# Batch 0's transposes in four PSUM banks instead of two, and a new order of all work (gated recurrence, then an MLP mixer, one core)

## The chip, the core and the metric

The kernel runs on one core of a Trainium2 chip. The metric is device time in microseconds, the median of several executions; lower is better. One further execution was recorded by the hardware profiler, and every row below comes from that one.

## What is computed

Four batches, eight heads, 768 steps, head width 48. First a recurrence with a decaying 48x48 state per head, then an MLP mixer over tokens and over channels:

```
for t in range(S):                                   # S = 768
    state = alpha[t, :, None] * state + outer(k[t], v[t])
    y[t]  = q[t] @ state
x  = y of all heads side by side                     # [4, 768, 384]
h  = relu(x^T @ w_tok1) @ w_tok2                     # w_tok1 768x256, w_tok2 256x768
u  = x + h^T
out = u + relu(u @ w_ch1) @ w_ch2                    # w_ch1 384x1536, w_ch2 1536x384
```

## The kernel before

**The recurrence by chunks.** A batch is cut into six chunks of 128 steps. The logarithm of alpha (`la`, on ACT) is summed along the chunk by matmuls (`cum`), the sums become two exponentials on ACT (`ek` and `eq`), and k and q are multiplied by them (`pkk` on POOL; `pkq` on DVE in batch 0 and on POOL later). TensorE (PE) transposes both (`tr`), the transposes are copied out of PSUM (`tp`, to the tiles `tk2`/`tq2` or `tkq`), and their products (`gt`) are masked on DVE (`gm`) and applied to v (`y`). The state of the chunk before comes in by `inter`, and the new state is made by `state`, `st` and `ss`. The result of a chunk is `x`. The three pairs of batch 0 and the first two pairs of batch 1 are "paired": two chunks at a time with interleaved steps. The other chunks are "natural": one at a time.

**The mixer.** `tok1` (L602 after batch 0) multiplies all six `x` by `w_tok1`, `ht` is its relu, `tok2` (L651) multiplies by `w_tok2`, `u` adds `x` on DVE, `utp` transposes and `ut` copies out. Batch 0 does this by another route (L582, L629, L634) that ends in `ut` as well. Then `ch1` (L691) makes 24 pieces of the hidden layer, `rt` is their relu, `ch2` (L715, three parts for each of six row blocks) brings them together, `o` copies out and `out` stores. The `ch1` and `ch2` of one batch are independent of the recurrence of the next batch, and they are put between its instructions.

**Weights.** All weights arrive in fp32 and are cast to bf16 by ACT, DVE or POOL: `wc1` in two halves of three casts each, `wc2` in four pieces (the casts are numbered 154, 156, 158, 160 in the table below).

**The order.** Nothing is scheduled at build time. Every piece of work gets a number when the graph is built, and the table `ORDER` lists these numbers in the order in which they are issued. A letter behind a number names the engine (A for ACT, D for DVE, P for POOL), the digits behind a dot are the PSUM banks, and `f` with a bank is a filler: one matmul of zeros, whose result nobody reads. The fillers all stand ahead of the first `ch1`. Each engine carries out its own instructions strictly in that order, so an instruction that waits holds back all behind it on its engine. Loads and stores are issued by SP, in the order of the table too.

**The transposes of batch 0.** For each pair and each of k and q there is one PSUM bank. The transposes of both chunks go into it, chunk `s` at column `512 * s`. Two copies take them out: of k one chunk each, of q two of the four head pairs of both chunks each. Of the two copies of one bank one goes to ACT and one to DVE. Between two engines that read the same bank a wait is placed.

Of the kernel before, what the change touches and what calls it, by code (L numbers as in the profile page):

```python
# [17 lines left out]
FUSE = 99  # L18
FETCH, BLOCK, AHEAD, ARRIVES = 193, 256, 449, (4.5, 30.0, 3.0)
# [6 lines left out]
0 1 f0 2 f0 f0 f0 f0 f0 3 f0 f0 f0 f0 f0 4 28 f0 29 f0 f0 30.0 5 31.1 32 f2 f2 38 6 f2 35 f2 33 f2 f2 f2 39 f2 34 f2  # L26
36 40 f2 43.2 41 7 f3 66 47.3 f4 65 48 44 49A 50D f4 67.4 46A 45D 68.5 69 f6 51.67 75 72 54.01 8 70 52 f3 f3 76 f3 73
f3 77 f3 80.3 78 f2 9 84.2 56 f6 85 105 81 71 f6 104 87D f6 f6 10 86A f6 f6 83D 106.6 82A 55 107.5 108 53 91.14 11 114
88.23 92 f0 42P 37A f0 f0 109 90 f0 58.07 115 89 57.13 60A 93 f2 116 12 f2 f2 59 f2 f2 f2 112 f2 111 63 61 117 14
123.2 64A f0 62 f0 124 74A 79P 119.0 110 16 120 125D 126A f4 94.41 122A 121D 18 96 127.57 97 130.36 95.20 128 113A  # L30
118P 100 132 98 102 133.4 99A 20 131 13P f5 103A 169.5 101 163.6 24 166.2 f3 15P 129 141.3 135 142.0 143 136 134.17
17P 137 139 145 138D 147 140A 144 146 259 148 150 149 151 19D 152 172.4 178.1 162A 161D 175.7 f0 173 176 174A 167 177D
260 164 168A 170 22D 21P 165A 179 f0 171A 23D f0 261 f0 180A f0 189.0 201.3 190A 195.4 262 202A 181.7 27D 25P 196A
185.2 26D 182A 153 193.6 186A 211.5 264 194D 223.1 263 212D 227.0 224A 265.3 228A 266.4 155 267 217.7 273 270 207.2
274 209.6 268 300 208D 218A 276 213.5 210D 215.1 214A 269 187.0 301 271 216A 203.4 188A 219.3 275 204A 302 225.2 220A
154D 199.7 272 226A 278.65 277 279 200A 303 221.1 280D 281A 156P 183.0 222A 282 283 184A 292.43 284D 285A 197.2 304
294 286.71 157 305 198D 289.05 205.6 287 306.4 288 206A 159 191.2 308 291 307.7 309 311 239.6 296 314 343 290 315
249.1 297 192D 293.54 344 312 319.37 298 295A 345 254.0 316 299A 234.2 158A 346 317 244.5 347 310 313 160D 240 318 348
245 351 241 349 320 352.4 242A 321D 246 322A 354 235 247D 353 350 358 236 356 243 323 362 324 237D 333.64 357 325A
326D 376.5 238 363.2 335 250 248 355 364 336 486 365 327.37 251 487 329 366 367 330.62 328 252A 488 255 332 368 256  # L40
339 369 359.73 331 257A 370.12 340 229.4 361A 360D 253 372D 371A 377 373.60 258 510 334.73 375 489 381.21 341 490 374
337 230 342A 378 382 338A 491 379.5 383 231 380A 492 384.0 232D 511.6 385A 493 513 388.3 512 516 233 386.2 389A 514
517 494 521 495 515 387D 522.7 390.1 496 523 398.5 391 524 394.4 526 396.0 399 392.6 395 400.3 527 535.2 393 518.17
401 497 402.54 528 519A 397 529.63 525 403A 553.1 404D 498 520A 536 405.05 530A 416.4 499 554 406A 440.7 407D 555 531A
500 417D 420.2 539 434.6 421D 441A 501 532.10 435A 550.53 534 422.4 502 430.2 551 546 423A 540.7 533 431A 452.6 558
552 442.0 541 537.5 453D 503 542 438.4 544 538D 559.2 439A 556.1 443D 504 560 543 412.3 545 557D 561 426.6 413D 505
432.7 564 427A 410.5 506 433A 446.4 562 411A 565 408.0 507 447A 563 572.1 577 450.2 409D 508 454.3 573 451A 547.67 574
455D 566.54 509 548A 578.0 549D 591.1 568A 567D 448.2 720 592 580 424.3 584 449D 579 588.76 583 721 425A 569.54 590
418.1 596 582 436.2 570 419A 414.0 571 437A 581 597.3 593 589 722 610.6 575.5 598 444.1 415D 599 601 723 576A 594.2
611 445A 481.4 595D 602 724 744 428.7 476.0 600 429A 725 603 604.35 612 585.61 605A 726 466.2 587D 586A 477 727 606A  # L50
482 728 607.73 751 615.16 609 483 729 755 616 471.5 608 478 617 613.3 730 479 472 614A 484 618.1 480 762 456.7 619D
473 485 773 622.6 731 474 732 620.0 623A 475 457 621A 733 458 734 634.3 459 630.4 735 628.1 635 632.5 631 624.6 780
460 626.0 629 461.7 625 792 736 627 462 737 633 463 636.34 738 464 639.16 637A 467 638D 640A 641D 465 468 799 774.0
469 745.5 775 793.7 656.4 746 778 747 756.3 470 650.6 795 739 757 749 684.1 651D 740 758 644.2 685D 776 748 662.5 794
760 645D 741 660.6 811 663D 657A 678.3 750 742 661D 787.0 769.1 679A 812.7 770 759 668.2 743 777 813 761 672.5 788 814
664.4 669A 673D 789 670.6 665A 666.3 779 671A 646.1 830 667D 682.0 798 647A 831.7 683A 806.2 781.54 797 832 807 763.63
833 752.10 765D 658.2 783A 835 754D 764A 674.7 753D 659D 782A 686.3 808 675D 800.40 687A 803.16 796 802D 816 784.25
801A 766.73 804 680.0 768 818 654.4 681A 836 767 648.1 655A 844.3 786 642.0 649A 817 771.7 785 822.41 643A 652.5 772A
805 834 837 790.2 824 815 653A 809.0 791A 823 838.76 810A 819.51 825.2 839D 820A 828.4 840D 676.0 821A 826 715.7 829D
827 677A 849.65 841.21 845 716 843 846 700.4 851 695.0 850 696 842 852.3 688.1 853D 847.5 689A 705.6 848D 697 854.2  # L60
698 699 717 855A 710.3 718 711 701 719 702 856.1 703 704 712 857A 690.5 713 858.0 714 868.2 859 862.7 860.4 869 864.1
863 866.3 691 861 867 692 865 706 693 873.02 694 870.74 874A 875D 707 871D 872A 910.3 708 894.1 911A 709 880.5 895A
908.2 881D 906.0 909A 912.7 907A 900.4 913A 876.6 901A 896.3 877A 918.1 897A 914.5 919D 904.2 915A 922.0 905D 902.7
923D 920.4 903A 898.6 921A 916.3 899A 888.1 917A 890.5 889A 884.2 891D 878.0 885A 886.7 879A 882.4 887A 892.6 883D
929.3 893A 939.1 930 931 940 932 944.5 933 945 946 934.2 947 941 948 924.0 942 925 943 926 935 927 936 928 949.7 937
950 938 951 954.4 955 952 956 953 957 958
# [12 lines left out]
class Graph:  # L79
# [5 lines left out]
    def add(self, name, costs, emit, reads=(), writes=(), prio=0, dma=None, new=(), tail=0.0, rows=False, loose=False, n=0, late=0.0):  # L85
        self.ops.append(Op(costs, emit, new))
        return self.ops[-1]
# [6 lines left out]
def kernel(  # L94
# [12 lines left out]
    nc = tc.nc  # L107
# [73 lines left out]
    gm_t = many("gm", 2 * NG, [128, 4, 128])  # L181
    ss_t = many("ss", NSS, [128, H, D])
    x_t = many("x", NX, [128, HD])
    ht_t = many("ht", 2 * NDT, [128, HD])
# [19 lines left out]
    def load_input(dst, src, service, keys, prio, loose=False):  # L204
        return g.add("load", {"SP": 0.06}, lambda e: nc.sync.dma_start(dst, src), writes=keys, prio=prio, dma=service, loose=loose)  # L205
# [629 lines left out]
```

## The time and the profile before

| | |
|---|---|
| time before, median of 3 | 174.6 us (173.99 to 174.98) |
| the profiled execution | 174.24 us, of which its span is 172.5 us |
| PE busy | 166.5 us (96%), 2099 matmuls, 61 of them fillers |
| DVE, ACT, POOL busy | 102.0, 96.0, 72.3 us |
| granted TensorE clock | 9 tenths or more in every slice |
| DMA | 9 tenths busy or more in most slices up to about 120 us |

A row of the timeline gives start, busy time, engine, line, operation, tiles written and read with their shapes, the count, and in brackets how long the engine had been idle and what released it. The busy time of a PE row reaches past the start of the next row, since matmuls overlap; how long a group holds PE is therefore read from the starts of two rows that follow each other.

### The profile page before, as it was taken

Reading aid. Unit: us, or ns where it says so; the run is one execution under the profiler, and the core shown is the slowest. Engines: PE = TensorE matmul, PEld = TensorE weight load, DVE = VectorE, ACT = ScalarE, POOL = GpSimd, SP = SyncE. Lnnn points to the kernel's source line nnn. Section 1 sums busy time; section 2 is a strip of 40 time slices with the busy share of each in tenths; the row PEclk is TensorE's granted clock in tenths of the full one; section 3 lists DMA queues with packets and bytes.
Section 4 is the critical chain, followed back from the end, with each engine's and each line's share of the span. In section 5 each row is a group of like instructions: output and inputs, shape, how many; then the busy total and the mean of one; then the engine's idle time right before and its main releaser. Section 6 shows DMA issues by size and latency. Waiting matters only on the chain.

```text
span 172.5 us, 5143 instructions
## 1 busy us (share of the span) xinstructions
PE 166.5 (96%) x2099; PEld 106.8 (62%) x2099; DVE 102.0 (59%) x212; ACT 96.0 (56%) x206; POOL 72.3 (42%) x114
## 2 busy tenths in 40 slices
PE   7999979999999999999999999999999999999993
PEld 3566656665666567566666665666676656656562
DVE  3159977544653597689593727495988248132231
ACT  2577552699865655497887231699771112865000
POOL 7252542319485782944877111499941000000000
PEclk9999999999999999999999999999999999999999
DMA  5999999999998999999999999995000221100133
GB/s 134 261 261 265 232 335 398 309 234 337 256 307 168 205 254 219 225 170 198 165 204 151 196 219 223 211 210 92 4 4 0 79 104 50 46 4 0 46 115 113
DMA packets 86150, 30.20 MB, mean 175 GB/s; under 512 B 79600, under 2 KB 85104, under 8 KB 86128
## 3 DMA queue, kind: packets, MB, share of 16 engines
q1 hardware_dynamic: 86128, 29.89, 75.2%
q8 instruction: 16, 0.26, 0.7%
q14 instruction: 6, 0.05, 0.1%
HBM read 25.17 MB, written 4.72 MB: 173 GB/s over the span
## 4 chain that ended last, share of the span: by engine, by line
PE 78%; DVE 6%; POOL 4%; DMA 3%; issue 3%; ACT 2%; SPq 1%; DVEq 0%; POOLq 0%
PE bank L691 27%; PE bank L715 23%; PE bank L289 4%; PE bank L651 3%; DMA ina<-in_alpha_dram 3%; PE bank L602 3%; DVE gm L309 2%; PE bank L387 2%; PE bank L338 2%; PE bank L423 2%; POOL pkk L275 2%; PE bank L521 1%; PE bank L411 1%; PE bank L352 1%; SPq L205 1%
## 5 line engine op out<-in xcount | busy, mean ns | idle before, releaser
L691 PE MATMUL bank<-ut,wc 128*128 128x384 bf16 x288 | 51.1, 326 | 0.0
L691 PEld LDWEIGHTS <-wc 128*128 128x128 bf16 x288 | 26.6, 98 | 16.5
L275 POOL TENSOR_TENSOR pkk<-ink,ek 128x384 bf16<-128x384 f32 x24 | 24.3, 1022 | 17.7 <-ACT ek L256 14.9
L715 PE MATMUL bank<-wc,rt 128*128 128x384 bf16 x144 | 26.5, 326 | 0.0
L715 PE MATMUL bank<-wc,rt_late 128*128 128x384 bf16 (+2 forms) x156 | 25.1, 314 | 0.0
L728 DVE TENSOR_TENSOR o<-bank,x 128x384 f32<-128x384 f32 (+2 forms) x19 | 10.1, 536 | 18.2 <-PE bank L715 18.2
L589 ACT ACTIVATE rt<-bank 128x384 bf16<-128x384 f32 x33 | 16.3, 494 | 7.4 <-PE bank L691 7.0
L282 POOL CAST vb<-inv 128x384 bf16<-128x384 f32 x21 | 10.5, 506 | 22.3 <-DMA inv<-in_v_dram 17.6
L715 PEld LDWEIGHTS <-rt_late 128*128 128x128 bf16 x156 | 14.4, 98 | 8.2
L275 POOL TENSOR_TENSOR pkq<-inq,eq 128x384 bf16<-128x384 f32 x18 | 17.9, 1003 | 2.8 <-ACT eq L258 2.8
L589 ACT ACTIVATE rt_late<-bank 128x384 bf16<-128x384 f32 x33 | 16.1, 495 | 5.3 <-PE bank L691 5.3
L309 DVE TENSOR_TENSOR gm<-bank,u 128x512 bf16<-128x512 f32 x28 | 17.3, 682 | 2.8 <-PE bank L387 2.6
L243 ACT ACTIVATE la<-ina 128x384 bf16<-128x384 f32 x24 | 12.1, 526 | 10.8 <-DMA ina<-in_alpha_dram 10.8
L715 PEld LDWEIGHTS <-rt 128*128 128x128 bf16 x144 | 13.2, 98 | 7.7
L792 PE MATMUL bank<-zeros 128*128 128x384 bf16 x61 | 15.1, 372 | 1.4 <-DVE la L192 1.2
L591 DVE TENSOR_SCALAR rt_late<-bank 128x384 bf16<-128x384 f32 x15 | 8.3, 554 | 10.0 <-PE bank L691 8.3
L309 DVE TENSOR_TENSOR gm<-bank,pmask 128x512 bf16<-128x512 f32 x20 | 12.7, 682 | 1.4 <-PE bank L521 1.3
L256 ACT ACTIVATE ek<-bank 128x384 f32<-128x384 f32 x24 | 11.4, 498 | 3.5 <-PE bank L355 2.0
L333 ACT CAST x<-bank 128x384 bf16<-128x384 f32 x16 | 7.3, 483 | 10.6 <-PE bank L338 9.4
L322 POOL TENSOR_TENSOR ss<-st,al 128x384 bf16<-128x384 f32 x12 | 10.0, 832 | 7.4 <-DVE st L319 5.4
L591 DVE TENSOR_SCALAR rt<-bank 128x384 bf16<-128x384 f32 x15 | 7.9, 554 | 5.3 <-PE bank L691 5.3
L297 ACT COPY tkq<-bank 128x512 bf16<-128x512 bf16 x17 | 9.3, 602 | 2.8 <-PE bank L289 2.7
(118 smaller groups left out, 237.3 us busy)
## 6 DMA issues: line engine op xcount, KB each, us to landing
out_dram<-o SPq DMA_DIRECT2D x23, 192.0 KB, 2.6
ina<-in_alpha_dram SPq DMA_DIRECT2D x14, 192.0 KB, 4.3
ink<-in_k_dram SPq DMA_DIRECT2D x14, 192.0 KB, 4.6
inq<-in_q_dram SPq DMA_DIRECT2D x14, 192.0 KB, 4.5
inv<-in_v_dram SPq DMA_DIRECT2D x14, 192.0 KB, 4.4
rt_late<-in_moe_w_ch_dram SPq DMA_DIRECT2D x2, 1152.0 KB, 10.1
rt_late<-in_moe_w_ch_dram SPq DMA_DIRECT2D x4, 576.0 KB, 7.1
ina<-in_alpha_dram SPq DMA_DIRECT2D x5, 384.0 KB, 6.3
```

Source lines behind the costliest of these rows:

```text
L243: g.add("la", {"ACT": 0.43}, lambda e: act.activation(la[:, :, 0:D], t, AF.Ln), key, [u["la"][1]], pr + 5)
L256: g.add("ek", {"ACT": 0.38}, lambda e: act.activation(ek, banks[bank.place][:, 0:HD], AF.Exp, scale=-1.0), [bank], [kek], pr + 4)
L275: lambda e, dst=dst, src=src, ex=ex: {"POOL": gps, "DVE": dve}[e].tensor_tensor(dst[:, :, 0:D], src, ex().rearrange("p (h d) -> p h d", h= ...
L282: lambda e: evict[e](vb, src), ksrc, [u["vb"][1]], pr + 4)
L309: g.add("gm", {"DVE": 0.60}, lambda e: dve.tensor_tensor(gm, banks[bank.place].rearrange("p (j t) -> p j t", j=4), wide(mask, [[0, 4], lis ...
L322: g.add("ss", {"POOL": 0.79}, lambda e: gps.tensor_tensor(ss, st.rearrange("p (h d) -> p h d", h=H), wide(al, [[1, 8], [0, D]]), ALU.mult) ...
L589: act.activation(dst, src, AF.Relu)
L591: dve.tensor_scalar_max(dst, src, 0.0)
L691: pe.matmul(banks[bank.place][:, 0:HD], lhsT=wc1[wp][:, kc, off : off + 128], rhs=ut_t[b % 2][:, kc, cs], start=(kc == 0), stop=(kc == NM ...
L715: pe.matmul(banks[bank.place][:, 0 : hi - lo], lhsT=rt_t[(b * NDC + mc) % NRT][:, i * 128 : i * 128 + 128], rhs=wc2[:, mc, lo:hi], start=( ...
L728: g.add("o", {"DVE": 0.09 + 0.38 * width}, lambda e, i=i, bank=bank, o=o, lo=lo, hi=hi: dve.tensor_tensor(o[:, lo:hi], banks[bank.place][: ...
L792: pe.matmul(banks[place][:, 0:HD], lhsT=zeros[:, 0:128], rhs=zeros, start=True, stop=True, skip_group_check=True)
```

## The change

**Four banks.** In batch 0 each half that is copied out on its own now has its own bank: two for k (one for each chunk) and two for q (one for each half of the heads). The number of transposes, copies and bytes stays the same. The copies of one pair no longer share a bank.

```diff
-                bank = Bank()
+                tb = [Bank(), Bank()]
                 for s in range(2):
                     src, ksrc = us[s]["p" + w]
...
                         for j in range(4):
-                            pe.transpose(ps[:, 512 * s + 128 * j :][:, 0:128], src[:, 2 * j : 2 * j + 2, :], id128)
-
-                    g.add("tr" + w, {"PE": 0.225}, emit, [ksrc], [bank], pr + 2, new=[] if s else [bank])
+                            part, at = (s, 128 * j) if w == "k" else (j // 2, 256 * s + j % 2 * 128)
+                            pe.transpose(banks[tb[part].place].bitcast(BF16)[:, at : at + 128], src[:, 2 * j : 2 * j + 2, :], id128)
+
+                    mine = [tb[s]] if w == "k" else tb
+                    g.add("tr" + w, {"PE": 0.225}, emit, [ksrc], mine, pr + 2, new=mine if w == "k" or s == 0 else [])
                 for part in range(2):
-                    def evicted(e, w=w, bank=bank, part=part):
+                    def evicted(e, w=w, part=part, bank=tb[part]):
                         ps = banks[bank.place].bitcast(BF16)
                         if w == "k":
-                            evict[e](tk2[:, part], ps[:, 512 * part : 512 * part + 512].rearrange("p (j t) -> p j t", j=4))
+                            evict[e](tk2[:, part], ps[:, 0:512].rearrange("p (j t) -> p j t", j=4))
                         else:
                             evict[e](tq2[:, 2 * part : 2 * part + 2].rearrange("p j (t s) -> p (j t) s", s=2),
-                                     wide(ps[:, 256 * part : 256 * part + 1], [[1, 256], [512, 2]]))
+                                     wide(ps[:, 0:1], [[1, 256], [256, 2]]))
```

**Switches that are off.** The change also brings uneven loads (`UNEVEN`), a `y` in two parts (`SPLIT`) and a mask by way of ACT and POOL (`AROUND`). All three lists are empty, so none of them issues anything. Their code moves the later lines by some 20.

**The order.** The whole table is another one. Two lines of it:

```diff
-36 40 f2 43.2 41 7 f3 66 47.3 f4 65 48 44 49A 50D f4 67.4 46A 45D 68.5 69 f6 51.67 75 72 54.01 8 70 52 f3 f3 76 f3 73
+40 f2 43.2 41 7 47.34 66 f5 34 f5 45D 65 48 44.5 50A 49D f6 67.6 46A 68.7 69 51.10 75 54.24 72 53 f3 8 70 f3 f3 76 55
```

There are 63 fillers now instead of 61, again all ahead of the first `ch1`. SP issues its first 38 loads in the same order as before, which is everything up to the end of batch 1's input; the stores of batch 0 then stand a little earlier among the loads of batch 2.

DVE in batch 0, the first pair and the start of the second (`tq20`, `tk20` are the transposes of the first pair, `tq21`, `tk21` of the second, `gm` the masks; L481 and L479 are the copies of q and k). Before:

```order
L481 COPY tq20_151<-bank3_64 128x512
L479 COPY tk20_153<-bank2_63 128x512
L309 TENSOR_TENSOR gm0_155<-bank6_67,pmask0_97 128x512
L275 TENSOR_TENSOR pkq2_121<-inq1_108,bank4_65 128x8x48
L275 TENSOR_TENSOR pkq3_122<-inq1_108,bank5_66 128x8x48
L309 TENSOR_TENSOR gm3_158<-bank1_62,pmask1_98 128x512
L265 TENSOR_TENSOR al2_137<-bank4_65,bm_84 128x16
L481 COPY tq21_152<-bank2_63 128x512
L479 COPY tk21_154<-bank3_64 128x512
```

And now, where the copies are L496 for k and L498 for q:

```order
L496 COPY tk20_153<-bank2_63 128x512
L498 COPY tq20_151<-bank3_64 128x512
L325 TENSOR_TENSOR gm1_156<-bank0_61,pmask0_97 128x512
L325 TENSOR_TENSOR gm2_157<-bank2_63,pmask1_98 128x512
L284 TENSOR_TENSOR pkq2_121<-inq1_108,bank6_67 128x8x48
L274 TENSOR_TENSOR al2_137<-bank6_67,bm_84 128x16
L284 TENSOR_TENSOR pkq3_122<-inq1_108,bank7_68 128x8x48
L325 TENSOR_TENSOR gm3_158<-bank4_65,pmask1_98 128x512
L325 TENSOR_TENSOR gm0_155<-bank1_62,pmask0_97 128x512
L496 COPY tk21_154<-bank2_63 128x512
```

The copy of k now goes ahead of that of q, and of the second pair DVE keeps one copy of four; ACT has the other three. In the third pair it is also one for DVE and three for ACT, instead of two and two.

ACT in batch 1, around the `la` of its fifth chunk (`la2` from `ina1`, L243 before and L252 now; `wc2` is the cast of the second channel weight, L762 and L782). Before:

```order
L333 CAST x6_172<-bank5_66 128x384
L333 CAST x7_173<-bank4_65 128x384
L762 CAST wc2_219<-rt_late_184 128x1152
L243 ACTIVATE la2_117<-ina1_100 128x8x48
L725 COPY o2_199<-bank6_67 128x384
```

And now:

```order
L265 ACTIVATE ek0_127<-bank2_63 128x384
L267 ACTIVATE eq0_131<-bank2_63 128x392
L782 CAST wc2_221<-rt_late_186 128x1152 x2
L252 ACTIVATE la2_117<-ina1_100 128x8x48
L265 ACTIVATE ek2_129<-bank4_65 128x384
```

The fourth cast of `wc2` (number 160) stood on DVE and stands now on ACT, directly ahead of that `la`. The two `x` that stood ahead of the casts went to DVE.

PE ahead of the `cum` of the same chunk (L352 before, L368 now; L497 transposes k of the second pair, L715 and L735 are `ch2`, L542 and L559 are `state`). Before:

```order
L497 MATMUL bank3_64<-id128_77,pkk1_124 128x64
L497 LDWEIGHTS pkk1_124
L497 MATMUL bank7_68<-id128_77,pkk1_124 128x64
L352 LDWEIGHTS u128_72
L352 MATMUL bank4_65<-la2_117,u128_72 128x384
```

And now:

```order
L559 LDWEIGHTS pkk1_124
L559 MATMUL bank7_68<-vb3_144,pkk1_124 128x96
L735 LDWEIGHTS rt4_191
L735 MATMUL bank6_67<-wc2_221,rt4_191 128x384
L735 LDWEIGHTS rt5_192
L735 MATMUL bank6_67<-wc2_221,rt5_192 128x384
L735 LDWEIGHTS rt6_193
L735 MATMUL bank6_67<-wc2_221,rt6_193 128x384
L735 LDWEIGHTS rt7_194
L735 MATMUL bank6_67<-wc2_221,rt7_194 128x384
L368 LDWEIGHTS u128_72
L368 MATMUL bank4_65<-la2_117,u128_72 128x384
```

The `state` of the second pair moved from behind this `cum` to ahead of it, and stands between two parts of `ch2`. The transposes of k of that pair and one part of `ch2` moved from ahead of it to behind it.

More of the change, by code (lines that the diff above doesn't have):

```diff
@@ L18 @@
 FUSE = 99
+UNEVEN = ()
+SPLIT, AROUND = (), ()
 FETCH, BLOCK, AHEAD, ARRIVES = 193, 256, 449, (4.5, 30.0, 3.0)
@@ L31 @@
[L31 to L35, printed above, removed]
@@ L83, in __init__, with add @@
         self.ops = []
-    def add(self, name, costs, emit, reads=(), writes=(), prio=0, dma=None, new=(), tail=0.0, rows=False, loose=False, n=0, late=0.0):
+    def add(self, name, costs, emit, reads=(), writes=(), prio=0, dma=None, new=(), tail=0.0, rows=False, loose=False, n=0, late=0.0, banks=(), gates=()):
         self.ops.append(Op(costs, emit, new))
@@ L305, in s_transpose, with s_mask @@
         s_transposed(n, tb, dst, key, prio)
-    def s_mask(bank, mask, slot, prio):
+    def s_mask(bank, mask, slot, prio, around=False):
         gm = gm_t[slot]
+        if around:
+            raw = sc_t[slot % 2]
+            g.add("raw", {"ACT": 0.48}, lambda e: act.copy(raw, banks[bank.place].rearrange("p (j t) -> p j t", j=4)),
+                  [bank], [("raw", slot % 2)], prio)
+            g.add("gmp", {"POOL": 1.15}, lambda e: gps.tensor_tensor(
+                gm, raw, wide(mask, [[0, 4], list(mask.ap[1])]), ALU.mult), [("raw", slot % 2)], [("gm", slot)], prio)
+            return
         g.add("gm", {"DVE": 0.60}, lambda e: dve.tensor_tensor(
```

111 lines of the change are left out of this document (62 added, 49 removed).

## The prediction

> **What bounds the kernel now.** I read the page first, then the timeline of the first 33 us, then PE's starts from there to the end, then what SP, ACT and POOL wait for between 33 and 75 us.
>
> ```profile
> span 172.5 us, 5143 instructions
> PE   7999979999999999999999999999999999999993
> DMA  5999999999998999999999999995000221100133
> 146.31 11.70 PE bank L691 x72
> ```
>
> PE is full nearly everywhere, and late in the program it runs at its best: 72 matmuls in 11.70 us are 162.5 ns each. Fillers hide idle time in the first slices only, since none stands behind the first `ch1`. The DMA row is the second fact: the engines are full until about 120 us. So batch 0 is a chain of dependent steps, the rest is PE work, and data arrive at a pace of their own. What happens at the shared banks, and where the chain of batch 0 ends:
>
> ```profile
> 10.48 0.69 DVE L481 COPY tq<-bank 128x512 bf16<-128x512 bf16 x1 [1.36 <-ACT tq L481]
> 20.77 0.51 ACT L282 CAST vb<-inv 128x384 bf16<-128x384 f32 x1 [0.43 <-DMA inv<-in_v_dram]
> 21.80 0.59 ACT L481 COPY tq<-bank 128x512 bf16<-128x512 bf16 x1 [0.53 <-DVE tq L481]
> 22.29 0.59 ACT L479 COPY tk<-bank 128x512 bf16<-128x512 bf16 x1
> 22.91 0.42 DVE L479 COPY tk<-bank 128x512 bf16<-128x512 bf16 x1 [1.14 <-ACT tk L479]
> 23.39 0.64 PE L521 MATMUL bank<-tq,tk 48*64 48x128 bf16 x32 [1.03 <-DVE tk L479]
> 30.33 2.11 PE L634 MATMUL bank<-wt,ht 128*128 128x384 bf16 x12
> 30.73 0.83 POOL L756 CAST wc<-rt_late 128x768 bf16<-128x768 f32 x1 [3.63 <-DMA rt_late<-in_moe_w_ch_dram]
> 31.65 1.02 DVE L756 CAST wc<-rt_late 128x768 bf16<-128x768 f32 x2
> 32.92 1.30 PE L691 MATMUL bank<-ut,wc 128*128 128x384 bf16 x7
> ```
>
> The two engines take turns at each bank: DVE waits 1.36 us for ACT in the first pair and 1.14 us in the third, and the third pair's `gt` starts only at 23.39. The first `ch1` is at 32.92. It needs `ut` and the three casts of the first half of `w_ch1`, which landed at 30.73.
>
> **Part 1: batch 0.** With a bank for each copy the waits for the other engine go, in all three pairs; what is late next is read for the third. There ACT now makes three of the four copies, with the `vb` cast between the first and the other two. That cast cannot start before v lands at 20.77, so they run from 21.28, 0.49 us apart as the two ACT rows show, and end at about 22.3 (21.28 + 0.49 + 0.59 = 22.36). The last `gt` comes at 22.4 to 22.5 instead of 23.39: 0.9 us. The first pair's shorter wait does not add to that, since v and the `pkk` of the third pair set this place. `ht` and L634 follow with the same 0.9: 29.4 instead of 30.33. Then the weights stop it: from their landing at 30.73, two DVE casts of 1.02 us together end at 31.75. I take the first `ch1` at 32.0, a gain of 0.9; the ends are 31.8 (1.1) and no gain at all.
>
> **Part 2: the gain meets the loads.** SP's order is unchanged up to the end of batch 1's input.
>
> ```profile
> 48.77 4.31 SPq L205 DMA_DIRECT2D inq<-in_q_dram  x1
> 51.83 1.15 ACT L762 CAST wc<-rt_late 128x1152 bf16<-128x1152 f32 x1 [0.37 <-DMA rt_late<-in_moe_w_ch_dram]
> 53.42 1.11 DVE L762 CAST wc<-rt_late 128x1152 bf16<-128x1152 f32 x1 [3.48 <-DMA rt_late<-in_moe_w_ch_dram]
> 54.11 0.52 ACT L243 ACTIVATE la<-ina 128x384 bf16<-128x384 f32 x1 [1.13 <-DMA ina<-in_alpha_dram]
> 55.28 0.29 PE L497 MATMUL bank<-id,pkk 64*128 64x64 bf16 x8
> 55.51 0.34 PE L352 MATMUL bank<-la,u 128*128 128x384 bf16 x1
> 58.01 0.52 ACT L243 ACTIVATE la<-ina 128x384 bf16<-128x384 f32 x1 [0.87 <-DMA ina<-in_alpha_dram]
> 58.07 0.50 PE L542 MATMUL bank<-vb,pkk 64*128 64x96 bf16 x16
> 58.65 0.34 PE L411 MATMUL bank<-vb,pkk 128*128 128x96 bf16 x4
> 59.84 0.42 PE L521 MATMUL bank<-tq,tk 48*64 48x128 bf16 x16
> 60.19 0.82 PE L715 MATMUL bank<-wc,rt 128*128 128x384 bf16 x4
> 60.94 0.42 PE L521 MATMUL bank<-tq,tk 48*64 48x128 bf16 x16
> 65.50 0.81 PE L715 MATMUL bank<-wc,rt 128*128 128x384 bf16 x4
> 66.15 0.36 PE L423 MATMUL bank<-vb,gm 128*128 128x48 bf16 x8
> ```
>
> One issue of SP takes 4.31 us, because the queue is full; ACT and DVE wait for data at 51.83, 53.42, 54.11 and 58.01. A batch 0 that ends 0.9 us earlier does not make these land earlier. In the new order the cast that waits until 53.42 stands on ACT, directly ahead of the fifth chunk's `la`. Queued behind it are that `la`, its `ek` and `eq`, and on PE everything behind the `cum`. The cast ends at 53.42 + 1.15 = 54.57, the `la` at 55.09, so the `cum` comes at 55.15; before it was at 55.51.
>
> When does PE get there? Before, it needed 55.51 - 32.92 = 22.59 us from the first `ch1`. One part of `ch2` (66.15 - 65.50 = 0.65) and the second pair's transposes of k (0.25, about the 0.23 of the half at 55.28) have moved behind the `cum`, and `state` has moved ahead of it (58.65 - 58.07 = 0.58, less 0.14 of overhead: 0.44). That is 0.46 less, and one more half-height group adds 0.2 (below). So PE arrives at 32.0 + 22.59 - 0.46 + 0.2 = 54.3 and waits 0.85. Of the 0.9 gained, 0.36 is left on the clock, and 0.46 of work is now behind this place: PE stands 0.1 us worse than before. Had batch 0 gained nothing, PE would arrive at 55.2 and the result would be nearly the same; an error in part 1 costs little.
>
> **Changes between full and half-height matmuls.** Four L715 take 0.65 us between full-height neighbours (65.50 to 66.15) and 0.75 ahead of a 48-row group (60.19 to 60.94). The way in costs 0.1, and the way out about as much. Behind the first `ch1` the old order has 24 runs of such groups and the new one 27, counted in the two orders: one more ahead of that `cum`, none between it and batch 1's `tok1`, one up to that batch's `ch1`, and one behind. The second and third add 0.2 each; the bounds are 0, where PE waits there anyway, and 0.6 for all three. The Trainium skill, "TensorEngine Tiling (Array Packing)", Key Properties, says that a change of tiling mode drains TensorE; the trace agrees with the 0.10 just shown. Taken by that rule, none of the three is free, and the sum would be 0.6 instead of 0.4.
>
> **Part 3: the end of batch 1's recurrence and its mixer.**
>
> ```profile
> 64.19 0.40 PE L387 MATMUL bank<-tkq 48*128 48x128 bf16 x8
> 64.43 0.56 PE L554 MATMUL bank<-vb,gm 64*128 64x48 bf16 x32
> 67.60 0.33 PE L352 MATMUL bank<-la,u 128*128 128x384 bf16 x1
> 67.86 2.11 PE L602 MATMUL bank<-x,wt 128*128 128x384 bf16 x12
> 68.57 0.49 ACT L256 ACTIVATE ek<-bank 128x384 f32<-128x384 f32 x1
> 70.32 1.95 POOL L275 TENSOR_TENSOR pkk<-ink,ek 128x384 bf16<-128x384 f32 x2
> 70.62 2.11 PE L651 MATMUL bank<-ht,wt 128*128 128x384 bf16 x12 [0.22 <-DVE ht L591]
> 71.15 2.88 DVE L657 TENSOR_TENSOR x<-bank,x 128x384 bf16<-128x384 f32 x6 [0.57 <-PE bank L651]
> 74.22 0.66 PE L289 MATMUL bank<-id,x 64*128 64x64 bf16 x18
> 74.81 1.48 PE L691 MATMUL bank<-ut,wc 128*128 128x384 bf16 x8
> ```
>
> From the `cum` to `tok1` PE is full in both orders, so `tok1` starts at about 67.86 + 0.1. From there to the first `ch1` of batch 1 it took 6.95 us, of which about 1.0 is waiting along `tok1`, `ht`, `tok2`, six `u` (2.88), `utp`, `ut`. The new order puts the next batch's `state` and `tr` between `tok1` and `tok2`, where PE waited. That `tr` needs `ek` and two POOL products. Before, `ek` was the second of two exponentials and ended at 68.57 + 0.49 = 69.06; now it is the first, 0.4 earlier and so 1.1 behind the `cum` of 67.60. Two products of 0.98 follow (1.95 for both), so `tr` can start 3.1 to 3.2 behind the `cum`, 2.9 behind `tok1`. With its 0.35, `tok2` is at 3.3 instead of 2.76 behind `tok1`. The chain behind it is as long as before, less some waiting that goes, and ends 0.35 later; in exchange a `gt` (64.43 - 64.19 = 0.24) is already done. Net +0.1, which includes this stretch's extra group only in part; the bounds are -0.9 (all waiting filled) and +0.5 (nothing of the work counts).
>
> **The sum.** 0.1 at the `cum`, 0.1 in the mixer, 0.2 for the last extra group: +0.4 us, no gain. On the profiled execution, 172.5 of span plus 1.7 around it, that is 174.24 + 0.4 = 174.6; it stands 0.4 below the median of 174.6, so the median comes to **175.0**. The tail (last `ch2`, `o`, store) has the same last steps, and I cost it at nothing. A measurement of this kernel can tell about 0.5% from no change, 0.87 us: faster means below 173.73, slower above 175.47.
>
> **The rivals.**
>
> *The gain stays* (0.20). The `cum` is not held, because the weight lands some tenths before 53.42 or PE arrives later than I think, and the work put between `tok1` and `ch1` fills the 1.0 of waiting there. Then -0.9 from batch 0, -0.6 from the mixer and +0.5 for the extra groups give -1.0: 173.6. For it speaks that all waits at the shared banks do go; against it the full DMA row and the data wait at 58.01, from which only 9.85 us lead to `tok1` through `cum`, `ek`, `pkk`, `pkq`, `tr`, `gt`, `gm`, `y` and `x`.
>
> *DVE comes too late in batches 2 and 3* (0.35, slower). A `y` needs two masks on DVE:
>
> ```profile
> 11.55 0.64 PE L521 MATMUL bank<-tq,tk 48*64 48x128 bf16 x32 [0.36 <-DVE tk L479]
> 12.07 0.69 DVE L309 TENSOR_TENSOR gm<-bank,pmask 128x512 bf16<-128x512 f32 x1 [0.58 <-PE bank L521]
> ```
>
> The first mask starts 0.52 behind the start of `gt`, two of them take 1.3, so `y` can follow 1.85 after `gt` if DVE is free. In the old order three parts of `ch2` (1.95) and a second `gt` stand between that `gt` and `y` in the last pair of batch 2's chunks; now there are two parts, 1.3 + 0.24 + 0.24 = 1.78. One `u` or `o` on DVE ahead of the masks turns this into a wait of up to half a microsecond. Twelve chunks lie in batches 2 and 3; at 0.1 to 0.15 each, 1.2 to 1.8 us come on top of 0.4: 176.2 to 176.8. It decides from about 0.04 us for each chunk, which brings the sum above 0.87. Against it: DVE is busy for only 102.0 of the 172.5 us.
>
> *The copies still wait for each other* (in the forecast's chance). Then batch 0 gains nothing, PE is at the `cum` at 55.2, and the time is 175.0 to 175.1 as well.
>
> **How the numbers follow.** The forecast of no change has 0.45, with a range of its own from 174.0 to 175.5. The rival that gains has 0.20, the slower one 0.35. To leave out no more than 2 in 10 the range goes to 173.5 on the side of the gain and to 176.5 on the other.
>
> **What would show it right or wrong.** Right: no copy of `tk` or `tq` in batch 0 waits for the other engine, the third pair's last `gt` is at 22.4 to 22.5, the first `ch1` at 31.8 to 32.1, and ACT shows a cast at 53.4 with the fifth chunk's `la` right behind it and a PE wait at that `cum`, at 55.1 to 55.2; `tok1` at 67.9 to 68.1. Wrong: a first `ch1` at 32.9 or later, a `cum` at 54.5 with PE running through, or batch 1's `ch1` more than 0.5 us away from 74.8; for the slower rival, PE waits for DVE behind 80 us.

## The result, and the profile after

The changed kernel takes 175.26 us, the median of 19 executions (173.94 to 176.32), the kernel before 174.13 (20 executions, 173.79 to 175.44). All medians, ranges and ratios here leave out a few disturbed executions. The ratio is 1.0038, with a 95% interval from 1.0020 to 1.0056: +0.66 us, above the 0.5% line only at its upper end, so "no change" at a small loss. Both kernels scatter by more than a microsecond, so the size of the loss depends on how it is taken: the means differ by 0.63 (175.08 and 174.44), near the ratio, the medians by 1.13. The profiled execution took 175.31 us, its span 173.6, which is 1.1 more than before.

The page of the changed kernel:

```profile
span 173.6 us, 5153 instructions
PE   7989999899999999999999999999999999999993
DMA  5999999999997998999998999995000105100133
PE 60%; SPq 12%; DMA 10%; POOL 7%; issue 6%; DVE 2%; ACT 1%; POOLq 0%; DVEq 0%; ACTq 0%
```

PE and DMA look as full as before. What is new is the last row, the shares of the chain that ended last: SP's queue and DMA, that is, data, have 22% of it. On the page of before the same row read:

```profile
PE 78%; DVE 6%; POOL 4%; DMA 3%; issue 3%; ACT 2%; SPq 1%; DVEq 0%; POOLq 0%
```

Batch 0, from the timelines of ACT, DVE, PE and POOL (start, duration, then what it waited for):

```profile
20.02 0.58 ACT L496 COPY tk<-bank 128x512 bf16<-128x512 bf16 x1 [0.80 <-PE bank L488]
20.50 0.51 ACT L291 CAST vb<-inv 128x384 bf16<-128x384 f32 x1
20.92 0.58 ACT L498 COPY tq<-bank 128x512 bf16<-128x512 bf16 x1
21.40 0.59 ACT L496 COPY tk<-bank 128x512 bf16<-128x512 bf16 x1
20.90 0.68 DVE L498 COPY tq<-bank 128x512 bf16<-128x512 bf16 x1
21.95 0.64 PE L538 MATMUL bank<-tq,tk 48*64 48x128 bf16 x32
29.22 2.11 PE L654 MATMUL bank<-wt,ht 128*128 128x384 bf16 x12
30.71 1.66 DVE L776 CAST wc<-rt_late 128x768 bf16<-128x768 f32 x2
30.74 1.22 POOL L776 CAST wc<-rt_late 128x768 bf16<-128x768 f32 x1 [2.55 <-DMA rt_late<-in_moe_w_ch_dram]
32.43 1.80 PE L711 MATMUL bank<-ut,wc 128*128 128x384 bf16 x10 [0.45 <-DVE wc L776]
```

No copy waits for the other engine any more; the two waits left, 0.48 in the second pair and 0.80 in the third, are for PE's own transposes. The third pair's `gt` comes at 21.95 instead of 23.39, 1.44 earlier. At L654 (L634 before) 1.11 of that is left (29.22 instead of 30.33), at the first `ch1` 0.49 (32.43 instead of 32.92): the casts of `w_ch1` hold it. Then batches 1 and 2:

```profile
52.27 1.15 ACT L782 CAST wc<-rt_late 128x1152 bf16<-128x1152 f32 x1 [0.54 <-DMA rt_late<-in_moe_w_ch_dram]
54.52 0.52 ACT L252 ACTIVATE la<-ina 128x384 bf16<-128x384 f32 x1 [1.10 <-DMA ina<-in_alpha_dram]
55.10 0.32 PE L368 MATMUL bank<-la,u 128*128 128x384 bf16 x1 [0.24 <-ACT la L252]
67.92 2.11 PE L622 MATMUL bank<-x,wt 128*128 128x384 bf16 x12
68.73 0.50 POOL L291 CAST vb<-inv 128x384 bf16<-128x384 f32 x1 [2.00 <-DMA inv<-in_v_dram]
70.25 0.34 PE L427 MATMUL bank<-vb,pkk 128*128 128x96 bf16 x4 [0.22 <-POOL pkk L284]
75.44 0.82 PE L711 MATMUL bank<-ut,wc 128*128 128x384 bf16 x4
87.44 0.50 POOL L291 CAST vb<-inv 128x384 bf16<-128x384 f32 x1 [1.10 <-DMA inv<-in_v_dram]
111.42 0.65 PE L711 MATMUL bank<-ut,wc 128*128 128x384 bf16 x3
```

The `cum` of the fifth chunk, `tok1` of batch 1 and its `ch1` are where the prediction put them (55.15, 67.96, about 75.3). But what holds PE at the `cum` is the `la`'s own load, not the cast ahead of it, and POOL waits for v until 68.73 and 87.44.

### The profile page after: what moved, and what is told of

It reads as the page before. It is cut to its first block, busy times and chain, and to the rows that moved or that the text cites. A ratio compares the mean times of both kernels' runs of the same rounds, so it can differ in the third digit from the quotient of the medians.

```text
span 173.6 us, 5153 instructions
## 1 busy us (share of the span) xinstructions
PE 167.3 (96%) x2101; PEld 105.8 (61%) x2101; DVE 99.4 (57%) x210; ACT 99.5 (57%) x208; POOL 71.4 (41%) x114
## 2 busy tenths in 40 slices
DMA packets 86150, 30.20 MB, mean 174 GB/s; under 512 B 79600, under 2 KB 85104, under 8 KB 86128
## 3 DMA queue, kind: packets, MB, share of 16 engines
q1 hardware_dynamic: 86128, 29.89, 74.8%
## 4 chain that ended last, share of the span: by engine, by line
PE 60%; SPq 12%; DMA 10%; POOL 7%; issue 6%; DVE 2%; ACT 1%; POOLq 0%; DVEq 0%; ACTq 0%
PE bank L735 23%; PE bank L711 22%; SPq L210 12%; DMA rt_late<-in_moe_w_ch_dram 6%; DMA ina<-in_alpha_dram 5%; PE bank L671 3%; PE bank L298 3%; POOL pkk L284 2%; PE bank L622 2%; POOL pkq L284 2%; POOL ss L338 2%; PE bank L403 1%; PE bank L439 1%; PE bank L427 1%; PE bank L368 1%
## 5 line engine op out<-in xcount | busy, mean ns | idle before, releaser
L284 POOL TENSOR_TENSOR pkk<-ink,ek 128x384 bf16<-128x384 f32 x24 | 23.7, 997 | 14.9 <-ACT ek L265 12.0
L735 PE MATMUL bank<-wc,rt 128*128 128x384 bf16 x144 | 27.0, 326 | 0.0
L735 PE MATMUL bank<-wc,rt_late 128*128 128x384 bf16 (+2 forms) x156 | 25.1, 314 | 0.0
L609 ACT ACTIVATE rt_late<-bank 128x384 bf16<-128x384 f32 x40 | 19.3, 496 | 5.8 <-PE bank L711 5.6
L252 ACT ACTIVATE la<-ina 128x384 bf16<-128x384 f32 x24 | 12.1, 525 | 16.3 <-DMA ina<-in_alpha_dram 16.3
L735 PEld LDWEIGHTS <-rt_late 128*128 128x128 bf16 x156 | 14.5, 98 | 8.4
L325 DVE TENSOR_TENSOR gm<-bank,u 128x512 bf16<-128x512 f32 x28 | 17.8, 683 | 2.2 <-PE bank L403 1.6
L735 PEld LDWEIGHTS <-rt 128*128 128x128 bf16 x144 | 13.0, 98 | 7.4
L611 DVE TENSOR_SCALAR rt<-bank 128x384 bf16<-128x384 f32 x23 | 12.3, 556 | 6.9 <-PE bank L711 5.8
L812 PE MATMUL bank<-zeros 128*128 128x384 bf16 x63 | 14.3, 354 | 1.2 <-DVE la L195 1.2
L609 ACT ACTIVATE rt<-bank 128x384 bf16<-128x384 f32 x25 | 12.2, 490 | 5.1 <-PE bank L711 4.9
L349 ACT CAST x<-bank 128x384 bf16<-128x384 f32 x18 | 8.5, 482 | 7.4 <-PE bank L354 6.2
L677 DVE TENSOR_TENSOR x<-bank,x 128x384 bf16<-128x384 f32 x18 | 8.7, 549 | 3.7 <-PE bank L671 3.7
L306 ACT COPY tkq<-bank 128x512 bf16<-128x512 bf16 x13 | 7.4, 591 | 3.8 <-PE bank L298 3.7
```

What stands on the lines that cost most here:

```text
L252: g.add("la", {"ACT": 0.43}, lambda e: act.activation(la[:, :, 0:D], t, AF.Ln), key, [u["la"][1]], pr + 5)
L284: lambda e, dst=dst, src=src, ex=ex: {"POOL": gps, "DVE": dve}[e].tensor_tensor(dst[:, :, 0:D], src, ex().rearrange("p (h d) -> p h d", h= ...
L325: g.add("gm", {"DVE": 0.60}, lambda e: dve.tensor_tensor(gm, banks[bank.place].rearrange("p (j t) -> p j t", j=4), wide(mask, [[0, 4], lis ...
L609: act.activation(dst, src, AF.Relu)
L611: dve.tensor_scalar_max(dst, src, 0.0)
L735: pe.matmul(banks[bank.place][:, 0 : hi - lo], lhsT=rt_t[(b * NDC + mc) % NRT][:, i * 128 : i * 128 + 128], rhs=wc2[:, mc, lo:hi], start=( ...
```

## The experiments

The theory: the gain of batch 0 is real; the new order behind it asks for data earlier than the old one, and the data, not PE's work, take the gain back. The rival: the new order itself is slower on PE, ACT or POOL. In a table order, one number is one operation; the letter is its engine, the digits behind the point its banks.

**1. The new order up to a point, the old one behind it.** Operations have the same numbers in both orders, so the table can be joined at a point: at the first `ch1`, at `tok1` of batch 1, and at the end of batch 2's token mixer. The first joint as a diff against the new order:

```diff
 f1 174D f1 181.1
-187.5 182A 262 195.2 188D 26A
+189.0 201.3 190A 195.4 262 202A
```

*Joint at the first ch1.* 

> The new code and the new order up to the first ch1 (181 of batch 0), then every remaining operation in the old order, with the old engines and banks. Theory (the gain is partly swallowed at the loads, the rest is spent by the new order behind it): the first ch1 comes at 32.4 as in the changed kernel, 0.5 ahead of before; of that 0.5 the sixth chunk's cum keeps 0.2 to 0.3, because its la still waits for alpha until about 58.0 (la ends 58.5, cum at 58.6 instead of 58.83); the time is 0.2 to 0.3 us below before. Rival 'the loads set everything up to batch 1's tok1': tok1 of batch 1 stays at 67.8 to 67.9 and the time equals before within 0.1. Rival 'only the later order costs, the loads swallow nothing': tok1 at 67.4, the time 0.5 below before.

*Joint at tok1 of batch 1.* 

> The new order up to the first tok1 of batch 1, the old order from there. Theory: the new order of batch 1's recurrence uses up what the loads left, so tok1 of batch 1 is at 67.9 and, with the old mixer (6.95 us from tok1 to ch1), ch1 of batch 1 at 74.8 to 74.9; the time is that of before, 0.0 to +0.1. Rival 'the recurrence's order costs nothing, everything lies in the mixer and behind': 0.2 to 0.3 below before, as with the cut at the first ch1. Rival 'the cost lies all here': +0.6, the whole difference.

*Joint at the end of batch 2's token mixer.* 

> The new order up to the end of batch 2's token mixer (the ut of that batch), the old order from there to the end. Theory: batch 1's mixer adds 0.3 to 0.35 (tok1 to ch1 7.5 instead of 6.95, with a gt of 0.24 already done) and small waits in batch 2 another 0.1 to 0.3, so most of the difference is already made: +0.4 to +0.7 us. Rival 'the tail costs' (the exchange of ch1 and ch2 in batches 2 and 3): 0.0 to +0.2 here, and the rest comes only with the last piece.

| order new up to | median (executions) | lowest to highest | ratio to before, 95% |
|---|---|---|---|
| first `ch1` | 174.13 (12) | 172.72 to 175.10 | 1.0006 (0.9983 to 1.0029) |
| `tok1` of batch 1 | 174.52 (11) | 173.74 to 175.75 | 1.0035 (1.0011 to 1.0060) |
| end of batch 2's token mixer | 174.54 (11) | 173.28 to 175.63 | 1.0021 (0.9998 to 1.0045) |

Before took 174.03 beside them. By the medians, the loss comes with the new order of batch 1's recurrence, but the intervals overlap, so this does not place it; the first two kernels were slower than expected. One execution decides more than the medians do. The third kernel runs the same instructions as the changed one up to the end of batch 2's token mixer, and its profiled execution, of span 171.7, went like this on PE:

```profile
31.93 2.29 PE L711 MATMUL bank<-ut,wc 128*128 128x384 bf16 x13 [0.33 <-DVE wc L776]
54.19 0.33 PE L368 MATMUL bank<-la,u 128*128 128x384 bf16 x1
66.87 2.11 PE L622 MATMUL bank<-x,wt 128*128 128x384 bf16 x12
73.90 1.64 PE L711 MATMUL bank<-ut,wc 128*128 128x384 bf16 x9
109.78 0.65 PE L711 MATMUL bank<-ut,wc 128*128 128x384 bf16 x3
```

That is 1.54 us ahead of the changed kernel's profile at batch 1's `ch1`, with the same instructions; 0.50 of it stands already at the first `ch1`, whose weight landed at 30.25 instead of 30.74. The order alone cannot be the cause. The old order can lose in the same way: in the kernel joined at the first `ch1` it stands behind the joint, and there the alpha of the sixth chunk landed only at 58.86 (58.01 before). Its two waits around that chunk's `cum`, on PE:

```profile
58.45 0.34 PE L427 MATMUL bank<-vb,pkk 128*128 128x96 bf16 x4 [0.88 <-POOL pkk L284]
59.44 0.32 PE L368 MATMUL bank<-la,u 128*128 128x384 bf16 x1 [0.64 <-ACT la L252]
```

**2. Less to load.** Each of the four pieces of the second channel weight loads one block of three; the other two are never loaded, and the casts and matmuls run over them as they lie. So these lean kernels do not compute the output; they serve for the time alone:

```diff
-op = load_input(staged, src, 1.55, keys, 2000, loose)
+op = load_input(staged[:, 0:1, :], src[:, 0:1, :], 1.55, keys, 2000, loose)
```

*With the old code and order.* 

> The kernel before, with only a third of each of the four pieces of the second channel weight loaded (one 128-row block of three), so that all later loads find some 1.2 MB less ahead of them; the rest of that weight is not loaded, the casts and matmuls are unchanged. Theory (when data land sets the time of every order here, and the scatter between executions is that of the loads): PE of the kernel before has hardly a wait behind 33 us, so it gains little, 0.0 to 0.4 us below before, and its executions lie closer together. Rival (the order of PE, ACT and POOL sets the time): the same as before within 0.2 us.

*With the new code and order.* 

> The changed kernel with the same cut in the loads of the second channel weight. Theory: without the waits for data the new order is as fast as the old one behind the first ch1, so it keeps the 0.5 us of batch 0: tok1 of batch 1 at 34.9 to 35.0 us behind the first ch1 (35.49 in the changed kernel, 34.94 before), the time 0.6 to 1.0 us below before and 0.3 to 0.8 us below the lean kernel with the old order. Rival (the new order itself costs, by changes of half and full height, the mixer of batch 1 and POOL): 0.4 to 0.8 us above the lean kernel with the old order, as without the cut.

*With four banks and the old order.* 

> Four banks with the old order, and the cut in the loads of the second channel weight (a third of each piece is loaded, the rest of that weight is not). Theory (the banks are worth the 0.5 us that the first ch1 comes earlier, and only data take it back): 0.4 to 0.6 us below the lean kernel with the old code, whose median was 174.05, so 173.4 to 173.7, its executions as close together as those (0.4 us), and level with the lean kernel of the new order (173.59). Rival (the new order adds a gain of its own that four banks alone don't have): 174.0, as the lean kernel with the old code.

The profiles show 28.63 MB moved instead of 30.20. The issue of SP that took 4.31 us in the kernel before takes 2.01 in the lean kernel with the old order.

| less to load, with | median (12) | lowest to highest | ratio to before, 95% |
|---|---|---|---|
| old code and order | 174.05 | 173.76 to 174.16 | 0.9985 (0.9972 to 0.9998) |
| new code and order | 173.59 | 173.13 to 174.66 | 0.9971 (0.9951 to 0.9991) |
| four banks, old order | 173.66 | 173.59 to 174.91 | 0.9955 (0.9932 to 0.9979) |

The sign turns: the new order now has the lower median by 0.46, and seven of its twelve executions are below the lowest of the old. By the ratios the step is smaller (0.24), and their intervals overlap, so the times alone only suggest it. The kernel with four banks ran at another time, when before itself took 174.51 (174.28 beside the other two); by its ratio it gains 0.5 on the old code, as expected, but its executions lie 1.3 us apart instead of 0.4. PE in the two profiled executions, of spans 172.3 and 171.8, old order first:

```profile
32.79 1.46 PE L691 MATMUL bank<-ut,wc 128*128 128x384 bf16 x8
55.37 0.34 PE L352 MATMUL bank<-la,u 128*128 128x384 bf16 x1
67.59 2.11 PE L602 MATMUL bank<-x,wt 128*128 128x384 bf16 x12
74.53 2.12 PE L691 MATMUL bank<-ut,wc 128*128 128x384 bf16 x12
110.34 0.65 PE L691 MATMUL bank<-ut,wc 128*128 128x384 bf16 x3
```

```profile
32.04 2.29 PE L711 MATMUL bank<-ut,wc 128*128 128x384 bf16 x13 [0.26 <-DVE wc L776]
54.29 0.33 PE L368 MATMUL bank<-la,u 128*128 128x384 bf16 x1
66.97 2.11 PE L622 MATMUL bank<-x,wt 128*128 128x384 bf16 x12
74.02 1.64 PE L711 MATMUL bank<-ut,wc 128*128 128x384 bf16 x9
109.59 0.65 PE L711 MATMUL bank<-ut,wc 128*128 128x384 bf16 x3
```

From the first `ch1` to that of batch 2 both take 77.55 us. With its full loads the old order takes 77.69, the new one 78.99. For the old order's 77.69, and its end, the kernel before shows:

```profile
110.61 0.65 PE L691 MATMUL bank<-ut,wc 128*128 128x384 bf16 x3
```

Both orders run the same matmuls in this stretch (144 of `ch1` and 144 of `ch2`, for example) and the same behind it. So the new order has no more work up to there, and late data cost it 1.44 us in the profiled execution and the old one 0.14. The changed kernel and its lean form carry out the same instructions, so their starts on PE show where the 1.44 is lost:

| start on PE | full loads | less to load | apart |
|---|---|---|---|
| first `ch1` | 32.43 | 32.04 | 0.39 |
| `cum` of batch 1's fifth chunk | 55.10 | 54.29 | 0.81 |
| `cum` of its sixth chunk | 58.55 | 57.60 | 0.95 |
| `state` behind batch 1's `tok1` | 70.25 | 68.92 | 1.33 |
| `tr` of q behind it | 71.21 | 69.78 | 1.43 |
| a `cum` of batch 2 | 89.09 | 87.51 | 1.58 |
| the `state` behind it | 90.08 | 88.26 | 1.82 |
| `ch1` of batch 2 | 111.42 | 109.59 | 1.83 |

Everywhere else behind the first `ch1` the two run in step to within 0.05 us. The full loads make the difference: ACT waited for alpha before the `la` at 54.52, 57.97 and 88.52, POOL for v before the `vb` at 68.73 and 87.44 and so was late with the `pkk` and `pkq` behind them, and each of the six starts follows the end of its `la`, `pkk` or `pkq` by 0.05 or 0.06 us.

**3. The four banks alone.** The old order with the new code; the added banks get places that are free, and two fillers move to other banks:

```diff
-47.3 48 44
+47.37 48 44.0
```

> The new code with four banks, the whole order as before: q is copied ahead of k, engines as before; only the added banks got free places. Theory: the banks alone remove the waits, the order is not needed for that: no copy of tk or tq in batch 0 waits for the other engine, the third pair's last gt is at about 22.5 instead of 23.39, the casts of the first channel weight on DVE then run at the same time as POOL's and take 1.6 to 1.7 us for two instead of 1.02, and the first ch1 comes at 32.4; the time is 0.2 to 0.3 us below before. Rival 'the banks do nothing without the new order of copies': gt at 23.2 to 23.4, first ch1 at 32.9, the time of before. Rival 'the first ch1 comes the whole 0.9 earlier': 32.0.

Median 173.90 (173.34 to 175.30), ratio 0.9993 (0.9972 to 1.0014): no difference that can be told, though with less to load (above) it gains 0.5. PE in batch 0 and behind batch 1's `tok1`, and the casts of `w_ch1`:

```profile
22.93 0.64 PE L538 MATMUL bank<-tq,tk 48*64 48x128 bf16 x32
30.06 0.83 POOL L776 CAST wc<-rt_late 128x768 bf16<-128x768 f32 x1 [3.51 <-DMA rt_late<-in_moe_w_ch_dram]
31.19 1.02 DVE L776 CAST wc<-rt_late 128x768 bf16<-128x768 f32 x2
32.47 1.79 PE L711 MATMUL bank<-ut,wc 128*128 128x384 bf16 x10
69.79 0.32 PE L368 MATMUL bank<-la,u 128*128 128x384 bf16 x1 [0.43 <-ACT la L252]
```

The waits of one engine for the other are gone, and the first `ch1` comes at the forecast time, as early as with the whole change, but not in the forecast way. `gt` is 0.4 later than the 22.5, DVE comes to its casts only behind POOL's and takes 1.02 for them, not 1.6 to 1.7, and the weight landed 0.68 earlier than in the changed kernel.

**4. Other rows of SP.** Two tries to bring the awaited data earlier, each with the new order and with four banks and the old order. First, three alphas go ahead of the k, q and v that stood before them; then batch 0's stores (five in the new order, all six in the old) go behind eight loads of batch 2. SP's row of the new order, the first try:

```diff
-343 344 345 346 347 348
+343 347 344 345 346 348
```

and the second:

```diff
-238 233 486 243 487 488 248 489 490 491 492 493 253
+486 487 488 489 490 491 492 493 238 233 243 248 253
```

*Alphas first, new order.* 

> The changed kernel; in SP's row alone three loads stand earlier: the alpha of batch 1's sixth chunk directly behind the alpha of the fifth, and in batch 2 that of the second chunk behind that of the first, and that of the fourth behind that of the third. Theory: the la of these chunks no longer waits for its own load, so the waits at the sixth chunk's cum and behind batch 1's tok1 go, where the changed kernel lost 0.3 to 0.5 us; the wait of the fifth chunk stays. The time is 0.2 to 0.6 us below the changed kernel, about that of before. Rival (order): the time of the changed kernel, +0.6 against before.

*Alphas first, four banks and old order.* 

> Four banks with the old order, and the same three loads earlier in SP's row. Theory: the first ch1 at 32.4 to 32.5, no wait at the sixth chunk's cum nor at the cum behind batch 1's tok1 (0.43 us in the run with four banks alone); the time 0.3 to 0.6 us below before, faster than both kernels. Rival (order): as with four banks alone, 0.1 us below before.

*Stores late, new order.* 

> The changed kernel; in SP's row alone the first five stores of batch 0 stand behind the loads of batch 2's first two chunks instead of among them. Theory: the loads of those two chunks land 1 to 3 us earlier, so the waits behind batch 1's tok1 (la at 69.51, state at 70.25, 0.5 us from tok1 to ch1 over the 7.03 of a run without them) go; the wait of the fifth chunk stays. The time is 0.2 to 0.5 us below the changed kernel. Rival (whatever stands first in a full queue, something behind it is late by as much, as with alpha first): no gain, 0.4 to 0.8 us above before.

*Stores late, four banks and old order.* 

> Four banks with the old order, and the six stores of batch 0 behind the loads of batch 2's first two chunks. Theory: the wait of 0.43 us at the cum behind batch 1's tok1 goes, and the gain of batch 0 comes through: 0.3 to 0.5 us below before, faster than both kernels. Rival (a full queue only shifts the lateness): as with four banks alone, 0.1 us below before, or above it.

| | median (executions) | ratio to before, 95% |
|---|---|---|
| alphas first, new order | 174.81 (12) | 1.0044 (1.0014 to 1.0075) |
| alphas first, four banks | 175.20 (10) | 1.0041 (1.0011 to 1.0072) |
| stores late, new order | 175.54 (12) | 1.0052 (1.0017 to 1.0088) |
| stores late, four banks | 174.98 (10) | 1.0013 (0.9979 to 1.0048) |

None of the four shows the gain that was expected. The alphas first with four banks are slower than their rival said too (0.1 below before); the other three are near the times of their rivals. What the traces show is the reason given by the rival for the stores: in a full queue something else is late instead. With the alphas first it was v, on POOL and then PE:

```profile
69.98 0.50 POOL L291 CAST vb<-inv 128x384 bf16<-128x384 f32 x1 [3.20 <-DMA inv<-in_v_dram]
71.49 0.34 PE L427 MATMUL bank<-vb,pkk 128*128 128x96 bf16 x4 [1.42 <-POOL pkk L284]
```

With the stores late, the alpha of the sixth chunk, which stands ahead of what was moved, came latest of all (before: `la` at 58.01). SP, ACT and PE:

```profile
54.32 0.71 SPq L210 DMA_DIRECT2D ina<-in_alpha_dram  x1
59.59 0.52 ACT L252 ACTIVATE la<-ina 128x384 bf16<-128x384 f32 x1 [1.59 <-DMA ina<-in_alpha_dram]
60.16 0.32 PE L368 MATMUL bank<-la,u 128*128 128x384 bf16 x1 [1.38 <-ACT la L252]
```

From issue to `la` it took 5.3 us; in the kernel before, 4.1 (53.91 to 58.01).

**5. The casts of the first channel weight.** The changed kernel with the one cast of the first half that POOL did on DVE as well:

```diff
-22D 23P 165A 173 21D
+22D 23D 165A 173 21D
```

> The changed kernel with all three casts of the first half of the first channel weight on DVE (one of them was on POOL). Theory (DVE and POOL slow each other down when both cast from SBUF to SBUF): three casts of 0.51 us on DVE alone, 1.53 together, ending earlier than the two of 1.66 beside POOL, and the first ch1 0.1 us earlier against the landing of the weight than in the changed kernel (landing to ch1 1.69 there). Rival (the casts are slow for another reason, the weight landing piece by piece): three casts take 2.4 us or more, and ch1 comes 0.7 us later.

```profile
31.21 1.50 DVE L776 CAST wc<-rt_late 128x768 bf16<-128x768 f32 x3 [0.59 <-DMA rt_late<-in_moe_w_ch_dram]
32.76 1.47 PE L711 MATMUL bank<-ut,wc 128*128 128x384 bf16 x8 [0.79 <-DVE wc L776]
```

Three casts on DVE alone take 1.50, less than two beside POOL (1.66). The first `ch1` follows 1.55 behind their start, 1.72 in the changed kernel: 0.17 gained, somewhat more than expected. The weight itself landed 0.5 later in this execution, so the time of this single run (176.18) says nothing on the casts.

## Why the prediction was right or wrong

"No change" at a small loss came out as forecast. That 175.26 is so near to the 175.0 is in part luck: the forecast stood on 174.6 as the time of before, and twenty executions gave 174.13. A rise of 0.4 was forecast, and 0.66 by the ratio, or 1.13 by the medians, was measured. The steps held less well. Of the signs named for "right", the copies without waits, the wait of PE at the `cum` of the fifth chunk (55.10) and `tok1` (67.92) came; the third pair's `gt`, the first `ch1` and the cast at 53.4 did not. One sign named for "wrong" came: batch 1's `ch1` at 75.44 is 0.63 from 74.8, though the prediction's own steps put it at about 75.3.

The span of the profiled execution splits into six stretches of PE, worked out from the rows above and in the prediction:

| us from ... to | before | after | less to load, old | less to load, new |
|---|---|---|---|---|
| start to first `ch1` | 32.92 | 32.43 | 32.79 | 32.04 |
| to `cum` of the fifth chunk | 22.59 | 22.67 | 22.58 | 22.25 |
| to `tok1` of batch 1 | 12.35 | 12.82 | 12.22 | 12.68 |
| to `ch1` of batch 1 | 6.95 | 7.52 | 6.94 | 7.05 |
| to `ch1` of batch 2 | 35.80 | 35.98 | 35.81 | 35.57 |
| to the end of the span | 61.89 | 62.18 | 61.96 | 62.21 |

The difference of 1.1 is -0.49 in batch 0, +1.30 from there to batch 2's `ch1`, and +0.29 behind.

*Part 1, batch 0.* Right on the waits. The third pair's `gt` came 0.5 earlier than forecast: v was there when ACT came to it, so the `vb` cast started at 20.50 instead of 20.77, and the first copy behind it followed after 0.42 instead of 0.51. The mis-sized term is "two DVE casts of 1.02 us together": they took 1.66. Batch 0 ends earlier, so DVE is free before the weight lands and starts at the same moment as POOL, where before it came at 31.65, behind POOL's cast (30.73 and 0.83). That is 0.64 of the gain. The 1.66 stood in the profile of before, at 33.68, beside POOL's 1.22. So the first `ch1` hangs on this landing now. In the seven profiled executions with the new order of batch 0 and its engines it follows the start of POOL's cast by 1.68 to 1.77 us, and that start lies between 30.16 and 30.95.

*Part 2, the cum and the ACT cast.* The place was right, the cause was wrong, and the time was right by luck. The weight landed 1.15 earlier than in the row of before (52.27 instead of 53.42), so the cast moved to ACT held nothing: it ended at 53.42, and `la` then waited 1.10 for alpha. That alpha landed 0.41 later than before (54.52 instead of 54.11) and so, by chance, where the forecast had the `la` start behind the cast (54.57). The work moved across the `cum` was sized well: forecast -0.26 ahead of it (-0.46, and 0.2 for one group), -0.33 with less to load (22.25 against 22.58), and 12.68 against 12.22, so 0.46, behind it.

*The half-height groups.* The traces have 24 and 27 runs of such groups behind the first `ch1`, as counted. Forecast +0.2 for the first extra one, up to `tok1`; with less to load the first `ch1` to `tok1` is 34.93 against 34.80, +0.13. The second lies between batch 1's `tok1` and `ch1` (3 runs instead of 2), where the whole stretch is 0.11 longer. The third lies behind batch 2's `ch1` (7 instead of 6). With the same matmuls, that last stretch is 0.2 to 0.3 longer in the new order, and hardly moves with the loads: 62.18 and 62.21, against 61.89 and 61.96 and, in the kernel joined at batch 2 with the old tail, 61.92 (171.7 - 109.78). So the 0.2 for the last extra group fits in size and place; that this group is the whole cause was not tried.

*Part 3, the mixer of batch 1.* Forecast +0.35 with a `gt` of 0.24 already done. With less to load the stretch gives +0.11 (7.05 against 6.94), and the next one is 0.24 shorter (35.57 against 35.81), the size of the `gt`. The profiled execution shows 0.57 and then +0.18, because v lands at 68.73 and `pkk` follows it, and `la` and `pkk` are late again before 89.09 and 90.08.

*What the sum left out.* "The gain meets the loads" was taken as one wait at one place. The old order had a cushion of 0.88 at the fifth chunk (its `la` ended at 54.63, the `cum` ran at 55.51). The new one asks 0.49 + 0.33 earlier and has 0.06 left there, so a landing that is a little late reaches PE, at this place and at five others: 1.44 in the profiled execution. The forecast had no term for the five.

*The rivals.* "The gain stays" is what the new order up to batch 2's mixer, with the old tail, does when the data come early: 173.28 was reached, and the profile shown under 1 is nearly that. It isn't the usual execution (median 174.54), and the changed kernel itself never went below 173.94. "DVE comes too late in batches 2 and 3" did not happen: the two waits in batch 2 come from ACT and POOL behind loads of alpha and v.

*Open.* Why the same load lands up to a microsecond earlier or later from one execution to the next, and whether the new order, besides asking earlier, also makes data land later. With less to load, the new order's executions still spread over 1.5 us and the old one's over 0.4, which is not explained. Each trace is of one execution; how much of the other executions' time is late data is not shown. None of the kernels with full loads beat the kernel before by more than can be measured.

## What to carry to other kernels

Before counting a gain ahead of a full DMA queue, read for each later consumer the cushion between the landing of its data and its use; an order without cushions takes over the scatter of the loads and can lose by it although it runs the same matmuls. A part of one weight left out in both kernels helps to tell a slow order from late data; here the times alone only suggested it, and the starts on PE, compared instruction by instruction, showed it. Where two engines' casts are sized from rows in which each ran alone, look for a row in which they ran together.

## What was not expected of the hardware

DVE and POOL take turns when both cast from SBUF to SBUF. Two DVE casts take 1.02 alone. When DVE starts 0.03 ahead of POOL (30.71 and 30.74 above), DVE's two take 1.66 and POOL's one 1.22; the first of DVE's two takes 0.56, as alone, and the second, from 31.19, takes 1.18. When POOL starts first, as in the kernel joined at the first `ch1`, POOL loses nothing and DVE as much:

```profile
30.16 0.83 POOL L776 CAST wc<-rt_late 128x768 bf16<-128x768 f32 x1 [2.39 <-DMA rt_late<-in_moe_w_ch_dram]
30.22 1.65 DVE L776 CAST wc<-rt_late 128x768 bf16<-128x768 f32 x2
```

The Trainium skill, "SBUF — State Buffer", in the section on its two separate sides, says that the port pair which VectorE and GpSimd share is an exclusive lock, held for its whole instruction by whichever starts first, if the VectorE instruction is in a 2-port mode. No row here shows the mode of the casts, but their times agree with the lock: cast of DVE, cast of POOL, cast of DVE one behind the other end at 30.71 + 0.51 + 0.83 + 0.51 = 32.56 by their times alone, 32.37 as measured.

The landing of one load scatters more than the differences studied here: the `la` of the sixth chunk, which waited for its alpha, started at 57.97 in the changed kernel, 58.01 before and 59.59 with the stores late, with issues of SP within 0.4 us of each other (53.91 to 54.32). These are three kernels, with one execution each.
